# Two groups' gating moved out of PSUM and five pairs' exponentials written block by block: a new order for a chunked-attention and gated-convolution kernel

## The chip, the cores and the metric

The program runs on one core of one Trainium2 chip. The metric is device time in microseconds (us). The core has five instruction queues: TensorE (PE, matrix multiplies; its weight loads are shown as PEld), VectorE (DVE), ScalarE (ACT), GpSimd (POOL) and SyncE (SP), which issues the transfers. Each queue runs its instructions strictly in the order in which the program holds them; semaphores make one queue wait for another.

## The reference, cut to what matters

Attention inside chunks of 64 positions, then a gated causal convolution with two 512 x 512 matrices. Sizes: batch 8, 8 heads, 576 positions, head width 64; 8 x 576 = 4608 rows of width 512.

```python
scores = scale * (q_c @ k_c^T)                # per chunk of 64 and head
attn = exp(scores - max(scores))              # over the keys
attn = attn / (sum(attn) + 1e-09)
x = attn @ v_c                                # then heads side by side: rows x 512
gate_pre = sum over 5 taps of conv_w[k] * x shifted by 4-k rows (zeros before a batch)
gate = 1 / (1 + exp(-gate_pre))
out = (gate * (x @ w_val)) @ w_out
```

## The kernel before

The 4608 rows are cut into nine groups g of 512 rows. For each group the work is split into pieces with short names, and one long string, ORDER, lists all pieces of the whole program in one sequence. Every piece issues its instructions to fixed engines, in that sequence, so ORDER sets the queue of every engine. A letter D or G behind a name puts the piece on DVE or POOL instead of its usual engine. A second table, SLOTS, says for every tile of a ring (x, acc, ps, gate and so on) which of its buffers it takes; a buffer is taken again when the last reader of its former tile is done. All instructions are recorded by one helper, so in the profile all of them have its line, L160.

The pieces, with g the group, p the pair of head blocks (0 or 1), m and c blocks of 128 channels:

- Loads on SP: lq, lk, lv (q, k, v of a pair), lw (a quarter of a weight matrix), lc (convolution weights). st stores 128 rows of the result.
- Weights arrive as 64-bit numbers and are split into a high and a low part for the fp32r matmuls: w1 to w9, wa, wb, on DVE, ACT and POOL. v stands for w_val, o for w_out.
- S (PE): scores of a pair, tile s in PSUM, 128 x 1024, in two halves. mx (DVE): maximum of each of 16 blocks of 64 keys. sb (DVE): s minus the maximum, to the SBUF tile e_row. ex (ACT): one exp over all 1024 columns. sm (DVE): sum of each block, a 128 x 1040 reduction with the 1e-9 in its last column, and the reciprocal. nm (POOL): multiply by it, to en.
- T (PE): eight transposes to PSUM tile et. ec (ACT): copy to SBUF, eb. A (PE): times v, into two ps tiles u = 0, 1.
- xc, xr (ACT): copies of these to x (for the convolution) and, rounded, to xh. xd (DVE): the remainder, xl.
- k0 (ACT) and k .. 1 to k .. 4 (DVE): the five taps, in acc. sg (ACT): sigmoid, to gate.
- V (PE): x times w_val, four channel steps c of three matmuls each (xh with v_hi, xh with v_lo, xl with v_hi), in a ps tile. gm (DVE): gt = ps times gate.
- gr (ACT): gt rounded to gh. gd (POOL): the rest, gl. P (PE): times w_out, four steps c of three matmuls. oc (ACT): copy to o, which st stores.
- W: matmuls on a zero tile that nothing reads.

PSUM holds one s tile and one et tile (two banks each) and four ps tiles. V keeps its ps tile from its first matmul until gm has read it.

Of the kernel before, what the change touches and what calls it, by code (L numbers as in the profile page):

```python
# [514 lines left out]
```

## Time and profile before

| | |
|---|---|
| median of 3 runs | 305.24 us (304.71 to 305.42) |
| the profiled execution's own time | 305.96 us |
| span from its first to its last instruction | 304.2 us |
| mean granted TensorE clock | 0.988 of full speed |
| busy: PE, DVE, ACT, POOL | 274.9, 266.1, 185.2, 85.5 us |

How to read it. In the timeline a row begins with its start in us from the start of the span, then its length in us, then engine, line, operation, out<-in, and the count of equal instructions merged into it; in brackets stands the idle time of the engine before it and what ended it. A group of the list by shapes gives count, total busy us and mean ns of one, then the idle time before its instructions. A row's length counts from its own start to its own end; successive instructions of one engine overlap by some 0.07 to 0.1 us, and the matmuls by more, so what an instruction costs its queue is the distance to the next start. In a table of windows each engine has busy us and, in brackets, its number of instructions; PEclk is the granted TensorE clock.

### The profile page before, as it was taken

The numbers are of one execution on the slowest core, as the hardware profiler recorded it, in microseconds if no ns is written. First come the engines' busy times: TensorE is split into PE (matmuls) and PEld (weight loads), VectorE is DVE, ScalarE is ACT, GpSimd is POOL, SyncE is SP. The second block draws the span as 40 slices with busy tenths as digits, with TensorE's granted clock in tenths as the row PEclk, the third lists the DMA queues.
The fourth block names the chain that finished last, engine by engine and source line by source line (L and its number), as shares of the span: only waits on it lengthen the run. The fifth ranks groups of instructions, "written<-read, shape, count | busy, mean of one in ns | idle before, by whom it ended". The sixth has DMA issues, their size and how long they took to land.

```text
span 304.2 us, 7897 instructions
## 1 busy us (share of the span) xinstructions
PE 274.9 (90%) x3356; PEld 218.4 (72%) x3361; DVE 266.1 (87%) x374; ACT 185.2 (61%) x314; POOL 85.5 (28%) x77
## 2 busy tenths in 40 slices
...
DMA packets 14291, 42.47 MB, mean 140 GB/s; under 512 B 1712, under 2 KB 1712, under 8 KB 14256
## 3 DMA queue, kind: packets, MB, share of 16 engines
...
q14 instruction: 9, 0.07, 0.1%
...
## 4 chain that ended last, share of the span: by engine, by line
PE 57%; DVE 31%; DMA 5%; issue 4%; SPq 1%; ACT 1%; DVEq 0%; ACTq 0%
PE ps L160 50%; DVE acc L160 12%; PE s L160 4%; DVE gt L160 4%; DVE e_row L160 4%; DVE rs L160 3%; DVE mx L160 3%; DVE xl L160 2%; DMA kt<-in_k 2%; PE et L160 2%; DMA vt<-in_v 2%; DVE gate L160 1%; SPq L160 1%; DVE gl L160 0%; DVE v_lo L160 0%
## 5 line engine op out<-in xcount | busy, mean ns | idle before, releaser
L160 DVE SCALAR_TENSOR_TENSOR acc<-x,cw,acc 128x516 f32<-128x516 f32 (+1 forms) x144 | 113.1, 818 | 2.9 <-ACT acc L160 1.8
L160 POOL TENSOR_TENSOR gl<-gt,gh 128x512 fp32r<-128x512 f32 x24 | 32.7, 1365 | 149.5 <-ACT gh L160 149.5
L160 PE MATMUL ps<-xh,v_hi 128*128 128x512 f32 x144 | 59.5, 413 | 6.2 <-DVE xl L160 6.2
L160 PE MATMUL ps<-xl,v_hi 128*128 128x512 f32 x144 | 57.3, 398 | 3.1 <-DVE xl L160 3.1
L160 PE MATMUL ps<-o_hi,gh 128*128 128x512 f32 x144 | 58.4, 405 | 0.0
L160 PE MATMUL ps<-xh,v_lo 128*128 128x512 f32 x144 | 57.2, 397 | 0.0
L160 PE MATMUL ps<-o_lo,gh 128*128 128x512 f32 x144 | 56.9, 395 | 0.0
L160 PE MATMUL ps<-o_hi,gl 128*128 128x512 f32 x144 | 56.9, 395 | 0.0
L160 ACT ACTIVATE gate<-acc 128x512 f32<-128x512 uint32 (+8 forms) x72 | 30.3, 466 | 20.9 <-DVE acc L160 20.7
L160 POOL TENSOR_TENSOR en<-e_row,rs 128x1024 f32<-128x1024 f32 x16 | 32.4, 2022 | 23.0 <-DVE rs L160 22.5
L160 PEld LDWEIGHTS ps<-xh,v_hi 128*128 128x128 f32 x144 | 27.2, 189 | 13.1 <-DVE xl L160 6.6
L160 ACT COPY o<-ps 128x512 f32<-128x512 f32 x27 | 15.7, 584 | 32.1 <-PE ps L160 30.3
L160 PEld LDWEIGHTS ps<-xl,v_hi 128*128 128x128 f32 x144 | 27.2, 189 | 10.4 <-DVE xl L160 3.9
L160 PE MATMUL s<-kt,qt 64*64 64x64 f32 x1152 | 23.5, 231 | 12.3 <-DMA kt<-in_k 10.1
L160 PEld LDWEIGHTS s<-kt,qt 64*64 64x64 f32 x1152 | 20.8, 144 | 17.1 <-issue 15.5
L160 PEld LDWEIGHTS ps<-o_hi,gl 128*128 128x128 f32 x144 | 27.1, 188 | 6.5
L160 PEld LDWEIGHTS ps<-o_hi,gh 128*128 128x128 f32 x144 | 27.1, 188 | 6.5 <-issue 0.2
L160 PEld LDWEIGHTS ps<-xh,v_lo 128*128 128x128 f32 x144 | 27.4, 190 | 5.5
L160 PEld LDWEIGHTS ps<-o_lo,gh 128*128 128x128 f32 x144 | 27.1, 188 | 5.8
L160 ACT CAST gh<-gt 128x512 fp32r<-128x512 f32 x36 | 22.1, 618 | 13.7 <-DVE gt L160 13.5
L160 ACT ACTIVATE e_row<-e_row 128x1024 f32<-128x1024 f32 x18 | 19.1, 1061 | 17.8 <-DVE e_row L160 17.7
L160 ACT CAST xh<-ps 128x512 fp32r<-128x512 f32 x36 | 20.8, 592 | 14.8 <-PE ps L160 14.3
...
## 6 DMA issues: line engine op xcount, KB each, us to landing
...
```

The lines of the kernel that those rows point to most:

```text
L160: return tc.keep_in_program_order(fn(*args, **kwargs))
```

## The change

Only ORDER and SLOTS differ; the pieces' functions are the same in both files, and some of them were not used before. What the new order does:

- For pairs (0,1), (1,0), (1,1), (2,0) and (2,1) the pieces sb, ex and sm give way to ng, ea and rc. ng (DVE) multiplies the 128 x 16 maxima by -1/8. ea (ACT) is 16 ACTIVATE instructions of 128 x 64 that read s in PSUM, take a column of the maxima as bias, and write their row sums through the accumulator output. rc (DVE) adds 1e-9 to the 16 sums and takes the reciprocal.
- For groups 0 and 1 gm gives way to vc (ACT: copies the ps tile of V to SBUF) and gs (DVE; one of the eight on POOL): gt = that copy times gate.
- Other pieces change engine: ec of 0 0, 0 1 and 6 1, xc of the first group and other copies, some weight pieces, k0, nm and gd now stand on DVE where they stood on ACT or POOL, or the other way round. As a whole DVE has 15 gd (12 before), 4 nm (2), 7 oc (9), 6 xc (5); POOL has 14 nm (16) and 21 gd (24).
- Rings: gate has 8 buffers (6 before), o 3 (2), xh and xl 4 (3).
- All pieces are put in another sequence, the loads too.

```diff
...
-w2 v 2,sb 0 1,T 0 0,w4 v 2,ex 0 1,W 6,w4 v 3,w5 v 3,w7 v 2,sm 0 1,ec 0 0,w8 v 2,S 1 0 0,w6 v 3,A 0 0,w1 o 2,w1 o 0,
-gm 0 0,w8 o 1,mx 2 0,gr 0 0,V 0 2 0,k0 1 1,V 0 2 1,gdD 0 0,sg 0 3,V 0 2 2,xd 1 0 1,wa o 1,ec 1 1,V 0 2 3,gm 0 1,
...
+w7 v 1,S 0 1 1,w6 v 1,w3 v 2,W 15,ex 0 0,w8 v 1,mx 0 1,lq 1 1,w2 v 2,wa v 1,ng 0 1,sm 0 0,ea 0 1,nmD 0 0,w1 v 3,
+V 1 1 3,vc 0 1,gs 0 0,sg 0 1,S 3 1 0,k 1 2 1,S 3 1 1,sg 0 2,A 2 0,gs 0 1,gr 0 0,lq 4 1,vc 1 1,k 0 3 4,gr 0 1,
...
-    gate="0123450123450134343013250413250143201543021534201543",
+    gate="0123456701450623152473152064731526047315204673125046",
-    xh="012012012012021021",
+    xh="012301230123013201",
-    o="010110111110100110000110111001011010",
+    o="012020002212012021121021012012121201",
```

The functions that the new order calls:

```python
def ng(g, p):
    m = mxs[g, p]
    run(V.tensor_scalar, out=m, in0=m, scalar1=-SCALE, scalar2=None, op0=ALU.mult)

def ea(g, p):
    probs[g, p] = e_rows[next(e_slot)]
    rss[g, p] = r = tile_of("rs", [P, 16], F32)
    sb, m = flat(s_ps[g, p]), mxs[g, p]
    for j in range(16):
        run(S.activation, out=probs[g, p][:, j, 0:D], in_=sb[:, j], func=AF.Exp, bias=m[:, j:j + 1], scale=SCALE,
            accum_out=r[:, j:j + 1])

def rc(g, p):
    r = rss[g, p]
    run(V.tensor_scalar, out=r, in0=r, scalar1=1e-9, scalar2=None, op0=ALU.add)
    run(V.reciprocal, out=r, in_=r)

def vc(g, m, copy=S.copy):
    v_sb[g, m] = tile_of("gl", [P, T], F32R).bitcast(F32)
    run(copy, out=v_sb[g, m], in_=v_ps[g, m])

def gs(g, m, on=V):
    gt[g, m] = tile_of("gt", [P, T], F32)
    run(on.tensor_tensor, out=gt[g, m], in0=v_sb[g, m], in1=gate[g, m], op=ALU.mult)
```

DVE's queue at the softmax of pairs (0,1) and (1,0), before (the digit behind a tile's name is its buffer, the number behind the underscore its place in the program; rs is the row sums, xl the remainder of x):

```order
L160 TENSOR_REDUCE mx2_394<-s0_294 128x16
L160 TENSOR_TENSOR xl0_401<-ps0_312,xh0_371 128x2x256
L160 TENSOR_TENSOR e_row0_63<-s0_294,mx2_394 128x16x64
L160 TENSOR_SCALAR gt0_406<-acc1_130 128x512
L160 TENSOR_TENSOR v_lo_67<-gate5_201,gate4_199 128x512
L160 SCALAR_TENSOR_TENSOR gt0_406<-gate3_348,gt0_406 128x512
L160 TENSOR_REDUCE rs2_439<-e_row0_63 128x16
L160 RECIPROCAL rs2_439<-rs2_439 128x16
```

and now, at the same place:

```order
L161 COPY eb0_306<-et0_286 128x1024
L161 TENSOR_SCALAR rs0_265<-rs0_265 128x16
L161 RECIPROCAL rs0_265<-rs0_265 128x16
L161 TENSOR_REDUCE mx2_383<-s0_310 128x16
L161 TENSOR_SCALAR mx2_383<-mx2_383 128x16
L161 COPY x0_81<-ps1_350 128x2x256
L161 TENSOR_TENSOR gate5_212<-gt0_235,v_hi_65 128x512
L161 COPY x0_81<-ps0_349 128x2x256
L161 COPY eb1_435<-et0_418 128x1024
```

The 1024-column subtraction and reduction are gone from DVE; small operations on 16 columns and three kinds of copies stand there.

ACT's queue around the exps of pairs (1,0) and (1,1), before (eb is the copy of the transposes, xh the rounded x):

```order
L160 ACTIVATE e_row0_63<-e_row0_63 128x16x64
L160 ACTIVATE acc2_437<-x0_74,cw_69 128x512
L160 COPY eb1_459<-et0_427 128x1024
L160 ACTIVATE acc2_437<-x0_74,cw_69 128x512
L160 ACTIVATE gate4_504<-acc1_130 128x512
L160 COPY x0_74<-ps3_468 128x2x256
L160 COPY x0_74<-ps2_467 128x2x256
L160 CAST xh1_519<-ps2_467 128x2x256
```

and now:

```order
L161 ACTIVATE e_row0_63,rs2_398<-s0_310,mx2_383 128x64 x16
L161 CAST xh0_481<-ps0_349 128x2x256
L161 CAST v_hi_65<-gt0_437 128x512
L161 CAST xh0_481<-ps1_350 128x2x256
L161 ACTIVATE gate4_526<-acc1_187 128x512
L161 CAST xh1_533<-ps2_439 128x2x256
L161 COPY x0_81<-ps3_440 128x2x256
L161 ACTIVATE e_row1_64,rs1_539<-s0_483,mx0_528 128x64 x16
L161 CAST xh1_533<-ps3_440 128x2x256
```

The casts to xh, for which DVE's xl and then PE's V wait, stand directly behind 16 small ACTIVATEs in ACT's queue.

## Rows read from the trace of the kernel before

**Rows 1.** The page, busy time by engine.

```profile
PE 274.9 (90%) x3356; PEld 218.4 (72%) x3361; DVE 266.1 (87%) x374; ACT 185.2 (61%) x314; POOL 85.5 (28%) x77
```

**Rows 2.** Table of windows: window, length, busy us by engine, PEclk, DMA, GB/s.

```profile
40.00:50.00 10.00, 3.88 (x79) 2.65 (x78) 9.97 (x16) 4.00 (x8) 2.17 (x1) 0.87 0.01 2
50.00:60.00 10.00, 9.62 (x97) 7.77 (x98) 9.97 (x15) 7.58 (x12) 3.21 (x2) 0.79 0.72 245
...
170.00:180.00 10.00, 8.92 (x160) 7.25 (x159) 9.97 (x13) 8.20 (x17) 3.06 (x3) 1.00 0.68 230
...
220.00:230.00 10.00, 10.00 (x49) 8.21 (x48) 9.70 (x14) 6.31 (x13) 0.00 (x0) 1.00 0.49 182
```

**Rows 3.** Timeline of PE, 43 to 59 us, and the last matmul.

```profile
50.38 0.79 PE L160 MATMUL ps<-xh,v_hi 128*128 128x512 f32 x1 [6.20 <-DVE xl L160]
...
58.53 0.39 PE L160 MATMUL ps<-xh,v_hi 128*128 128x512 f32 x1
...
59.23 0.39 PE L160 MATMUL ps<-xh,v_hi 128*128 128x512 f32 x1
...
300.14 0.40 PE L160 MATMUL ps<-o_hi,gl 128*128 128x512 f32 x1
```

**Rows 4.** Timeline of DVE, 12 to 66 us.

```profile
11.99 1.23 DVE L160 TENSOR_REDUCE mx<-s 128x16 f32<-128x1024 f32 x1 [1.87 <-PE s L160]
...
48.38 0.68 DVE L160 TENSOR_TENSOR o_lo<-gate,gate 128x512 fp32r<-128x512 f32 x1
48.98 0.74 DVE L160 SCALAR_TENSOR_TENSOR acc<-x,cw,acc 128x512 f32<-128x512 f32 x1
49.64 0.68 DVE L160 TENSOR_TENSOR xl<-ps,xh 128x512 fp32r<-128x512 f32 x1
...
61.25 0.68 DVE L160 TENSOR_TENSOR gt<-ps,gate 128x512 f32<-128x512 f32 x1
61.84 1.41 DVE L160 TENSOR_SCALAR gt<-acc 128x512 uint32<-128x512 uint32 x1
...
65.52 0.69 DVE L160 TENSOR_TENSOR xl<-ps,xh 128x512 fp32r<-128x512 f32 x1 [0.29 <-ACT xh L160]
```

**Rows 5.** Groups by shape: count, busy us, mean ns, idle before.

```profile
L160 DVE TENSOR_TENSOR e_row<-s,mx 128x1024 f32<-128x1024 f32 x18 | 21.9, 1218 | 0.3
L160 DVE TENSOR_REDUCE rs<-e_row 128x16 f32<-128x1040 f32 x18 | 22.1, 1226 | 0.0
L160 DVE RECIPROCAL rs<-rs 128x16 f32<-128x16 f32 x18 | 4.6, 253 | 0.6
L160 DVE TENSOR_SCALAR gate<-gt 128x512 uint32<-128x512 uint32 x8 | 3.3, 410 | 0.0
L160 PE MATMUL s<-kt,qt 64*64 64x64 f32 x1152 | 23.5, 231 | 12.3 <-DMA kt<-in_k 10.1 <-DVE acc L160 1.1 <-PE ps L160 0.9
L160 PE MATMUL et<-ident,en 128*128 128x128 f32 x144 | 18.8, 273 | 0.9 <-POOL en L160 0.5 <-ACT eb L160 0.4
L160 ACT COPY o<-ps 128x512 f32<-128x512 f32 x27 | 15.7, 584 | 32.1 <-PE ps L160 30.3 <-issue 1.7
L160 ACT ACTIVATE e_row<-e_row 128x1024 f32<-128x1024 f32 x18 | 19.1, 1061 | 17.8 <-DVE e_row L160 17.7
L160 ACT ACTIVATE gate<-acc 128x64 f32<-128x64 f32 x8 | 2.0, 247 | 1.3 <-DVE acc L160 1.1
L160 ACT ACTIVATE gate<-acc 128x512 f32<-128x512 f32 x8 | 5.1, 637 | 4.9 <-DVE acc L160 4.9
L160 ACT ACTIVATE acc<-x,cw 128x512 f32<-128x512 f32 x7 | 4.8, 713 | 0.0
L160 ACT ACTIVATE cw_t<-cw_t 128x20 f32<-128x20 f32 x1 | 0.2, 220 | 0.7 <-DVE cw_t L160 0.7
```

**Rows 6.** Timeline of POOL, 60 to 63 us.

```profile
60.47 1.27 POOL L160 TENSOR_TENSOR gl<-gt,gh 128x512 fp32r<-128x512 f32 x1 [3.11 <-ACT gh L160]
61.70 1.27 POOL L160 TENSOR_TENSOR o_lo<-gate,gate 128x512 fp32r<-128x512 f32 x1
```

More of the change, by code (lines that the diff above doesn't have):

```diff
@@ new lines @@
+lk 4 1,w5 o 1,mx 1 1,lq 2 0,wa v 3,xr 0 1 0,xc 0 1 1,ng 1 1,xd 0 1 0,ea 1 1,nm 1 0,xd 0 0 1,xcD 0 1 0,w1 o 3,hl 1,
+T 1 0,wbD v 3,V 0 3 0,w4 o 1,W 2,wbD v 1,w7 o 1,V 0 3 1,w1 o 2,xr 0 1 1,w3 o 3,S 2 0 0,rc 1 1,w2 o 2,lw o 0,
+xd 0 1 1,S 2 0 1,nm 1 1,w6 o 1,w8D o 1,k0 0 2,V 0 3 2,lk 2 1,mx 2 0,lq 2 1,w2 o 3,V 0 3 3,lv 1 1,w5 o 2,W 4,lq 3 0,
+w4 o 3,ec 1 0,ng 2 0,k 0 2 1,k0 0 1,A 1 0,w7 o 3,ea 2 0,k 0 0 2,V 0 0 0,k 0 1 1,V 0 0 1,w8D o 3,V 0 0 2,waD o 1,
+k 0 1 2,k 0 2 2,w1 o 0,w3 o 2,xr 1 0 0,k 0 0 3,S 2 1 0,w6 o 3,S 2 1 1,rc 2 0,vc 0 3,xd 1 0 0,nm 2 0,V 0 0 3,lk 3 0,
@@ new lines @@
+xc 1 0 1,mx 2 1,lv 2 0,V 0 2 0,xr 1 0 1,lq 3 1,vc 0 0,T 1 1,xd 1 0 1,k0 0 3,waD o 3,ec 1 1,w4 o 2,wb o 3,w3 o 0,
+xc 1 0 0,A 1 1,k 0 0 4,w2 o 0,wb o 1,k 0 2 3,V 0 2 1,xr 1 1 0,lv 3 0,ng 2 1,w4 o 0,V 1 3 0,xr 1 1 1,k 0 3 1,ea 2 1,
+T 2 0,xd 1 1 0,V 0 2 2,k 0 3 2,V 1 3 1,xd 1 1 1,k 0 2 4,V 1 3 2,w7 o 2,V 1 3 3,k 0 3 3,V 0 2 3,w7 o 0,k 0 1 3,
+w5 o 0,S 3 0 0,w8D o 2,xc 1 1 0,S 3 0 1,rc 2 1,k0 1 0,w8D o 0,V 1 2 0,lk 3 1,xc 1 1 1,lq 4 0,mx 3 0,nm 2 1,V 1 2 1,
+w6 o 0,V 1 2 2,k0 1 1,sb 3 0,V 1 1 0,vc 0 2,k0 1 2,V 1 2 3,waD o 0,ec 2 0,V 0 1 0,k 1 0 1,V 1 1 1,vc 1 2,wbD o 0,
@@ new lines @@
+k0 2 2,k 1 3 1,P 0 3 0,k 1 0 4,oc 0 0,P 0 3 1,ec 3 0,k 1 3 2,st 0 0,P 0 3 2,lk 4 0,k 1 2 3,k0 2 1,P 0 3 3,k 2 0 1,
+sg 1 0,P 0 2 0,k 1 2 4,oc 0 3,P 0 1 3,k0 2 3,k 1 1 3,P 0 2 1,xr 2 1 1,k 1 3 3,oc 0 1,P 0 2 2,k 2 1 1,sg 1 2,st 0 1,
+P 0 2 3,gs 1 0,k 2 1 2,A 3 0,oc 0 2,k 1 1 4,gr 1 0,st 0 2,S 4 0 0,xr 3 0 0,lv 4 0,gs 1 2,S 4 0 1,sg 1 1,lv 3 1,
+k 1 3 4,V 2 1 0,lq 5 0,xd 2 1 1,V 2 1 1,hl 3,sg 1 3,k 2 1 3,V 2 1 2,gr 1 2,k 2 1 4,V 2 0 0,mx 4 0,gd 1 2,V 2 0 1,
+ex 3 1,V 2 0 2,xd 3 0 0,gsG 1 1,V 2 0 3,xc 3 0 1,sb 4 0,xr 3 0 1,V 2 1 3,gd 1 0,gr 1 1,xd 3 0 1,S 4 1 0,xc 3 0 0,
@@ new lines @@
+sm 3 1,S 4 1 1,ex 4 0,gd 1 1,P 1 3 0,P 1 2 0,gs 1 3,P 1 2 1,nmD 3 1,gr 1 3,P 1 3 1,P 1 3 2,sm 4 0,gd 1 3,T 3 1,
+sg 2 1,P 1 3 3,k 2 3 1,ec 3 1,gm 2 1,P 1 2 2,nm 4 0,oc 1 3,mx 4 1,P 1 2 3,A 3 1,oc 1 2,k 2 0 2,st 1 2,P 1 0 0,
+k 2 2 1,xc 3 1 0,lk 5 0,T 4 0,k 2 0 3,xr 3 1 0,gr 2 1,k 2 3 2,P 1 0 1,xc 3 1 1,xd 3 1 0,P 1 0 2,gd 2 1,k0 3 2,
+sb 4 1,P 1 0 3,V 2 3 0,k 2 3 3,oc 1 0,V 2 3 1,xr 3 1 1,k 2 2 2,st 1 0,V 2 3 2,k0 3 3,lv 5 0,k 2 3 4,lq 5 1,V 2 3 3,
+k 2 0 4,sg 2 3,V 2 2 0,k 2 2 3,sg 2 0,V 2 2 1,k 3 3 1,ec 4 0,V 2 2 2,gm 2 0,V 2 2 3,k0 3 0,k 3 2 1,gr 2 0,P 1 1 0,
@@ new lines @@
+k 2 2 4,P 1 1 1,k 3 3 2,sg 2 2,P 1 1 2,xd 3 1 1,hl 4,gd 2 0,gm 2 3,P 1 1 3,S 5 0 0,ex 4 1,gm 2 2,A 4 0,k 3 0 1,
+oc 1 1,S 5 0 1,gr 2 3,k 3 3 3,lv 4 1,V 3 3 0,k0 3 1,st 1 3,sm 4 1,gd 2 3,V 3 3 1,lq 6 0,xc 4 0 0,lk 5 1,xr 4 0 0,
+V 3 3 2,gr 2 2,k 3 3 4,V 3 3 3,xd 4 0 0,gd 2 2,P 2 3 0,mx 5 0,P 2 3 1,sg 3 3,nm 4 1,P 2 3 2,sb 5 0,xc 4 0 1,P 2 3 3,
+xr 4 0 1,V 3 0 0,xd 4 0 1,oc 2 3,k 3 1 1,T 4 1,st 2 3,k 3 0 2,V 3 0 1,ec 4 1,gm 3 3,V 3 0 2,k 3 0 3,A 4 1,k 3 2 2,
+S 5 1 0,k 3 1 2,xc 4 1 0,lv 5 1,S 5 1 1,k 3 0 4,xr 4 1 0,lk 7 1,V 3 0 3,xc 4 1 1,lk 6 0,xd 4 1 0,st 0 3,V 3 2 0,
@@ new lines @@
+xr 4 1 1,k 3 1 3,gr 3 3,V 3 1 0,mx 5 1,sg 3 0,gd 3 3,V 3 1 1,V 3 2 1,gm 3 0,k 3 1 4,V 3 1 2,gr 3 0,k0 4 2,sb 5 1,
+V 3 2 2,gd 3 0,P 2 1 0,xd 4 1 1,S 6 0 0,k 3 2 3,ex 5 1,S 6 0 1,k 3 2 4,V 3 1 3,lk 6 1,ex 5 0,sm 5 1,lq 6 1,V 4 3 0,
+V 4 3 1,sm 5 0,V 4 3 2,nm 5 1,sg 3 1,V 4 3 3,sg 3 2,V 3 2 3,mx 6 0,nm 5 0,k0 4 3,P 2 1 1,gm 3 1,P 2 1 2,gm 3 2,
+gr 3 1,P 2 1 3,sb 6 0,gr 3 2,hl 5,P 3 3 0,k0 4 0,T 5 1,gdD 3 2,k0 4 1,gdD 3 1,P 3 2 0,ec 5 1,k 4 3 1,P 3 3 1,oc 2 1,
+k 4 3 2,P 3 3 2,st 2 1,k 4 1 1,P 3 3 3,lq 7 0,k 4 2 1,T 5 0,oc 3 3,k 4 3 3,P 3 2 1,k 4 3 4,A 5 1,k 4 1 2,sg 4 3,
@@ new lines @@
+S 6 1 0,k 4 0 1,xc 5 1 1,S 6 1 1,xcD 5 1 0,P 3 2 2,lq 7 1,gm 4 3,xr 5 1 0,st 1 1,P 3 2 3,k0 5 2,lk 7 0,xd 5 1 0,
+P 3 1 0,lv 6 0,k 4 0 2,P 3 0 0,st 3 3,k0D 5 3,P 3 0 1,mx 6 1,ex 6 0,P 3 1 1,xr 5 1 1,k 4 0 3,P 3 1 2,ec 5 0,sm 6 0,
+P 3 1 3,oc 3 2,P 3 0 2,oc 3 1,st 3 2,xd 5 1 1,P 3 0 3,nm 6 0,sb 6 1,V 4 0 0,A 5 0,oc 3 0,k 4 0 4,ex 6 1,S 7 0 0,
+k 5 3 1,S 7 0 1,xc 5 0 0,k 5 2 1,xr 5 0 0,V 4 1 0,lk 8 1,k 4 2 2,xr 5 0 1,lv 6 1,V 4 1 1,k 4 1 3,xc 5 0 1,lq 8 0,
+T 6 0,xd 5 0 0,k0 5 0,V 4 1 2,k 4 2 3,gr 4 3,V 4 2 0,k 4 1 4,V 4 2 1,mx 7 0,gd 4 3,V 4 0 1,sg 4 1,V 4 0 2,xd 5 0 1,
@@ new lines @@
+ec 6 0,k 4 2 4,V 4 0 3,sg 4 0,k 5 3 2,V 4 2 2,sm 6 1,sg 4 2,P 2 2 0,V 4 1 3,gm 4 0,P 2 2 1,nm 6 1,sb 7 0,P 2 2 2,
+gr 4 0,k0 5 1,V 4 2 3,k 5 3 3,T 6 1,gdD 4 0,P 2 2 3,gm 4 2,S 7 1 0,k 5 1 1,gr 4 2,A 6 0,gm 4 1,gd 4 2,S 7 1 1,
+ecD 6 1,xr 6 0 0,V 5 3 0,lk 8 0,oc 2 2,hl 6,st 3 1,V 5 3 1,k 5 0 1,xc 6 0 1,st 2 2,V 5 3 2,k 5 3 4,lv 7 1,gr 4 1,
+xr 6 0 1,st 3 0,V 5 3 3,xcD 6 0 0,lq 8 1,sg 5 3,gdD 4 1,P 4 3 0,k0 6 0,gm 5 3,P 4 3 1,k 5 1 2,P 4 3 2,mx 7 1,
+P 4 3 3,P 4 0 0,xd 6 0 0,oc 4 3,P 4 0 1,sb 7 1,P 2 0 0,k 5 1 3,P 4 0 2,ex 7 0,k 5 2 2,P 2 0 1,gr 5 3,k 5 1 4,
@@ new lines @@
+P 2 0 2,ex 7 1,xd 6 0 1,P 2 0 3,k 5 0 2,V 5 1 0,oc 2 0,gdD 5 3,P 4 0 3,k0D 6 1,A 6 1,sm 7 0,sg 5 1,S 8 1 0,lv 7 0,
+S 8 1 1,xr 6 1 0,sm 7 1,nm 7 0,V 5 1 1,xr 6 1 1,xc 6 1 1,V 5 1 2,xd 6 1 0,oc 4 0,V 5 1 3,nm 7 1,xd 6 1 1,xc 6 1 0,
+st 4 0,V 5 0 0,mx 8 1,st 2 0,k0 6 2,P 4 1 0,gm 5 1,V 5 0 1,k 5 0 3,P 4 1 1,k 6 0 1,V 5 2 0,sb 8 1,T 7 0,V 5 0 2,
+k 5 0 4,V 5 0 3,k 5 2 3,sg 5 0,V 5 2 1,k0D 6 3,gr 5 1,k 6 3 1,V 5 2 2,ec 7 0,k 5 2 4,P 4 1 2,k 6 3 2,P 4 1 3,sg 5 2,
+gm 5 0,V 6 3 0,hl 7,gdD 5 1,gr 5 0,V 6 3 1,k 6 3 3,oc 4 1,V 6 3 2,st 4 1,k 6 3 4,V 6 3 3,st 4 3,gdD 5 0,sg 6 3,
@@ new lines @@
+A 7 0,k 6 0 2,S 8 0 0,gm 6 3,xr 7 0 0,V 5 2 3,k 6 0 3,xc 7 0 1,T 7 1,xd 7 0 0,xr 7 0 1,k 6 2 1,P 4 2 0,xc 7 0 0,
+ec 7 1,P 4 2 1,k0D 7 0,xd 7 0 1,P 4 2 2,k0 7 1,k 6 2 2,A 7 1,gm 5 2,k 6 1 1,S 8 0 1,gr 5 2,P 5 3 0,xr 7 1 0,gd 5 2,
+mx 8 0,xr 7 1 1,P 5 3 1,xc 7 1 1,xd 7 1 0,P 4 2 3,P 5 3 2,xd 7 1 1,xc 7 1 0,oc 4 2,k 6 2 3,P 5 3 3,k0 7 2,st 4 2,
+V 7 3 0,k 6 2 4,lv 8 1,k0 7 3,V 7 3 1,k 6 0 4,oc 5 3,V 7 3 2,k 7 3 1,gr 6 3,st 5 3,V 7 3 3,k 7 3 2,V 6 0 0,sb 8 0,
+gd 6 3,ex 8 1,V 6 0 1,V 6 0 2,sm 8 1,V 6 0 3,P 5 2 0,sg 6 0,k 7 3 3,V 6 2 0,gm 6 0,P 5 2 1,k 6 1 2,P 5 2 2,ex 8 0,
@@ new lines @@
+k 6 1 3,P 5 2 3,k 7 3 4,gr 6 0,V 6 2 1,oc 5 2,sm 8 0,V 6 2 2,st 5 2,V 6 1 0,lv 8 0,k 7 2 1,V 6 1 1,nmD 8 0,V 6 1 2,
+P 5 0 0,k 7 2 2,P 5 0 1,k 6 1 4,T 8 0,sg 6 1,hl 8,gd 6 0,V 6 1 3,ec 8 0,V 6 2 3,gm 6 1,sg 7 3,P 5 0 2,k 7 0 1,
+gr 6 1,P 5 1 0,nmD 8 1,sg 6 2,P 5 0 3,P 5 1 1,gm 7 3,gd 6 1,ocD 5 0,P 5 1 2,gm 6 2,A 8 0,gr 6 2,P 5 1 3,xcD 8 0 0,
+gr 7 3,gd 6 2,T 8 1,P 6 3 0,k 7 2 3,ec 8 1,P 6 3 1,k 7 0 2,oc 5 1,P 6 3 2,k 7 0 3,xc 8 0 1,st 5 1,P 6 3 3,st 5 0,
+k 7 0 4,k0 8 0,V 7 0 0,k 7 2 4,sg 7 0,V 7 0 1,k0D 8 1,xr 8 0 0,ocD 6 3,V 7 0 2,xr 8 0 1,xd 8 0 0,V 7 0 3,st 6 3,
```

122 lines of the change are left out of this document (34 added, 88 removed).

## The prediction, made before the changed kernel ran

> **What bounds the kernel now.** I read the busy sums first, then the table of windows and the timelines of the two engines that are full. PE is busy 274.9 of 304.2 us and DVE 266.1, ACT 185.2 [rows 1]. The windows show when: from 220 to 230 us PE is busy for all 10 us, while from 40 to 50 it is busy for 3.88, and DVE in that stretch for 9.97 [rows 2]. So the late part is set by PE, the early part by DVE: matmuls cannot start because the remainders xl that DVE makes come late. One such wait is 6.20 us, and the matmul behind it runs 0.79 us instead of 0.39, in a window with a granted clock of 0.79 [rows 2, 3]. From then on the program is a queue of PE work that has to be got through, up to 300.54 us [rows 3]. The time saved is therefore what the last late xl of the early part gains, less what PE then has more behind it.
>
> That point is the xl of group 1, second pair, second half (xd 1 1 1): DVE starts it at 65.52 us [rows 4]. Behind it, in both programs, stands one V step that needs it; all W matmuls stand ahead of it.
>
> **DVE ahead of that point.** The distance between starts is 0.60 us for a two-input operation of 512 columns (48.38 to 48.98) and 0.66 for a tap (48.98 to 49.64) [rows 4]. Operations of 1024 columns take 1.22 us [rows 5], less the same overlap of 0.08 us: 1.14. A sum with its reciprocal, 1226 and 253 ns [rows 5], comes to 1.43. Counted in both queues up to xd 1 1 1, the new one has less: 4 sb (4.6 us), 3 sm (4.3), 5 taps (3.3), 3 gm, one gd and one wb (5 x 0.60 = 3.0), together 15.2. It has more: one mx (1.1), two eb copies of 1024 columns from PSUM, priced like the subtraction that reads PSUM (2.3), three x copies and two w8 (3.0), one k0 (0.5), one weight step (0.3), and 13 operations on 16 columns, 5 in ng and 4 x 2 in rc. These have the reciprocal's row, 253 ns less overlap, 0.19 each: 2.5. Sum 9.7. Net 5.5 us less.
>
> By these prices DVE had 53.1 us of work ahead of that xl and began it at 65.52, so 12.4 us were lost: 6.0 before the first maximum at 11.99, whose wait for PE is in its row, and 6.4 in between. Part of the 6.4 is GpSimd: a TENSOR_SCALAR of 512 columns takes 1.41 us where its group has 0.41, beside a POOL operation from 61.70 to 62.97, while the PSUM reader in front of it, beside the POOL operation at 60.47, takes its usual 0.68 [rows 4 to 6]. In the new order the first maximum has 4.6 us of work before it and cannot come earlier than the same four 512 KB loads allow, so 7.4 are lost there. For the rest I followed the queue by hand.
>
> **The exps on ACT.** No row shows a 64-column ACTIVATE with bias column and accumulator. Nearest: 247 ns for 64 columns from SBUF; a column operand adds 713 - 637 = 76 ns at 512 columns; two neighbours overlap by 0.10 us; an accumulator output is at least free and at most a second instruction as long as a 20-column ACTIVATE, 220 ns [rows 5]. Bounds: 0.15 us (247 less overlap) and 0.47 (247 + 220). I take 0.30: 0.247 + 0.076 - 0.10 = 0.22 and 0.08 for the accumulator, nearer its cheap end because it writes one column. A pair then costs ACT 16 x 0.30 = 4.8 us instead of 1.06 [rows 5]. What hides it: ACT has idle time early, 6.0 of 10 us from 40 to 50 [rows 2]. What is queued behind it: the casts to xh, the copies to x and eb. DVE's xl waits for xh, PE's A for eb. Followed by hand at 0.30: ea 0 1 from 16.3 to 21.1, when DVE reaches rc 0 1 at 21.9; ea 1 0 from 23.9 to 28.7, xh at 29.2, when DVE is free at 29.0; ea 1 1 from 32.4 to 37.2, rc reached at 37.2; ea 2 0 from 42.1 to 46.9, rc reached at 47. The two engines meet within half a microsecond each time: the cover is just thick enough, and every 0.05 us more per instruction costs 3 pairs x 16 x 0.05 = 2.4 us before the point. On the walk DVE reaches xd 1 1 1 at 55.9; with 0.6 for the later start of the first maximum and 1.0 for collisions with POOL, 57.5. That is 8.0 earlier than 65.52: 5.5 of work and 2.5 of lost time.
>
> The Trainium skill, "ScalarE: Activation LUTs", What ACT_TABLE_LOAD costs, gives an ACTIVATE with a column bias about 280 ns + 0.833 ns per column, back-to-back ones overlapping by some 93. For 64 columns that is an estimate of 240 ns, without the accumulator; the 247 ns row agrees with the page's other form. By it a pair costs 3.8 us, ACT is never late, and only the 0.4 us by which it now holds DVE goes: 298.8.
>
> **PE behind that point.** Ahead of its V step the old queue had 18 V and 1 P steps, the new one 13 V: 6 more steps remain, each 0.70 us (58.53 to 59.23, three matmuls [rows 3]), 4.2 us. Half an S and one T fewer remain: 23.5 / 36 = 0.65 and 18.8 / 18 = 1.04 [rows 5]. Net 2.5 us more.
>
> **The rest.** vc adds 8 copies of 0.58 us [rows 5] to ACT and frees the ps tile without waiting for the sigmoid; off the path while ACT is not the bound. gs for gm: same 0.60 us if undisturbed; disturbed is a rival below. The longer rings only remove waits (bounds 0 and the half microsecond or so that a wait for a buffer would show). After the point I keep the losses of before, less 0.5 us: 46 long POOL operations instead of 53. The other engine moves there cancel: DVE's total by these prices falls by 1.6 us.
>
> **Sum.** -8.0 + 2.5 - 0.5 = -6.0 us. The profiled execution took 305.96 (span 304.2), 0.72 above the median 305.24. 305.24 - 6.0 = 299.2 us.
>
> **Rivals.**
> - ACT becomes the bound (slower). At 0.47 us an instruction a pair costs 7.5 us, 2.7 more; three pairs stand in series ahead of xd 1 1 1 (1 0, 1 1, 2 0): 8.2 us later, 307.4. It decides from 6.0 / 48 = 0.125 above 0.30, that is 0.425. For it: the cover is thin and a small instruction's time is nearly all fixed, 247 ns for 64 columns against 637 for 512 [rows 5]. Against: nothing in the rows makes a column's write cost as much as an instruction. 0.15.
> - GpSimd takes it back. The eight gs read two SBUF tiles where gm read PSUM. If the seven on DVE each meet a POOL operation, they stretch by about what was seen, up to 1.0 us each, 0.6 on average: 4.3 us, 303.5. For it: the 1.41 us row [rows 4, 6]. Against: gm's row beside POOL shows that POOL pieces can stand where DVE reads PSUM, and most of the early ones do in the new queue. The Trainium skill, "SBUF — State Buffer", Who interferes with whom, says that DVE operations with two SBUF inputs block against GpSimd operations that read SBUF, which speaks against gs; for one-input ones in a two-port mode it says the same, and the 1.41 us row agrees. 0.20.
> - All of it arrives. Exps at 0.25 or less and no collisions: DVE at 55.0 instead of 57.5, and 2.0 us of PE's idle time after 70 us go too (1.08 in the window of 170 to 180 alone [rows 2]): 294.7. 0.20.
> - It does nothing: the later groups, where DVE is as full as before, set the end whatever the start; 305. DVE still has all maxima, taps and remainders of groups 3 to 8. Against it: PE is busy for 10 us of 10 in the window of 220 to 230 [rows 2]. 0.05.
> - The forecast, 299.2, with its own range of 297 to 301.5: 0.40.
>
> **Chances and range.** No change means within 0.2%, 0.6 us, about what a measurement of this kernel can tell. Faster: 0.40 + 0.20 + 0.17 of the second rival = 0.77; same: 0.05; slower 0.18. The range of 8 in 10 leaves out most of the slower rival and the edge of the best: 293 to 305.
>
> **What would show it.** Right: the first long waits of PE for xl shrink; xd 1 1 1 starts at 56 to 59 us; 128x64 ACTIVATEs of e_row at about 0.3 us from start to start; PE without idle from 60 us on. Wrong: DVE or PE waiting for ACT's xh, eb or rs in the first 60 us with ACT full (first rival); gt<-gl rows far above 0.68 us beside POOL (second); PE idle after 70 us (fourth).

## The result and the profile after

The changed kernel takes 307.15 us (median of 12 runs, 305.48 to 308.74) where the kernel before takes 304.9 (12 runs). The ratio is 1.0068, 95% interval 1.0041 to 1.0095: slower by 0.7%. The forecast was 299.2. The profiled execution took 307.59 us with a span of 305.4.

The page, for [rows 1]: DVE has 9.3 us less, ACT 17.9 more, PE 6.3 more: 2.6 up to the end of xd 1 1 1, at a granted clock of 0.87 against 0.95 before, and 3.7 behind it.

```profile
PE 281.2 (92%) x3358; PEld 221.8 (73%) x3363; DVE 256.8 (84%) x380; ACT 203.1 (67%) x475; POOL 74.9 (25%) x71
```

The windows of [rows 2], and one more, 140 to 150 us.

```profile
40.00:50.00 10.00, 9.04 (x151) 6.16 (x152) 9.89 (x18) 9.68 (x43) 1.91 (x1) 0.89 0.63 207
50.00:60.00 10.00, 7.06 (x145) 5.97 (x146) 9.97 (x16) 8.17 (x26) 4.98 (x3) 0.83 0.58 217
140.00:150.00 10.00, 7.62 (x86) 6.13 (x85) 8.23 (x11) 8.18 (x12) 5.26 (x5) 0.83 0.53 195
170.00:180.00 10.00, 10.00 (x152) 8.46 (x145) 8.92 (x14) 8.93 (x17) 1.29 (x1) 1.00 0.47 162
```

ACT is now nearly full from 40 to 50, as its 16 small exps per pair make it. DVE is as full there as before. PE has no idle time from 170 to 180, where it had 1.08 us, but a hole from 140 to 150 that was not there.

DVE's timeline, for [rows 4]: the two operations of 16 columns that open rc, at 24 and 33 us; two places where a maximum is followed by ng; w8 at 43 us; an ng in its usual time; a weight step and two taps at 57 us; and the last late xl.

```profile
24.30 0.35 DVE L161 TENSOR_SCALAR rs<-rs 128x16 f32<-128x16 f32 x1
...
24.84 1.16 DVE L161 TENSOR_REDUCE mx<-s 128x16 f32<-128x1024 f32 x1
26.04 0.97 DVE L161 TENSOR_SCALAR mx<-mx 128x16 f32<-128x16 f32 x1
...
33.09 0.62 DVE L161 TENSOR_SCALAR rs<-rs 128x16 f32<-128x16 f32 x1
33.75 0.25 DVE L161 RECIPROCAL rs<-rs 128x16 f32<-128x16 f32 x1
33.92 1.16 DVE L161 TENSOR_REDUCE mx<-s 128x16 f32<-128x1024 f32 x1
35.11 1.80 DVE L161 TENSOR_SCALAR mx<-mx 128x16 f32<-128x16 f32 x1
...
43.00 2.00 DVE L161 TENSOR_TENSOR gate<-gate,gate 128x512 f32<-128x512 f32 x1
...
46.66 0.16 DVE L161 TENSOR_SCALAR mx<-mx 128x16 f32<-128x16 f32 x1
...
56.77 1.50 DVE L161 TENSOR_SCALAR gt<-acc 128x512 uint32<-128x512 uint32 x1
58.19 2.43 DVE L161 SCALAR_TENSOR_TENSOR acc<-x,cw,acc 128x512 f32<-128x512 f32 x2
...
63.14 0.68 DVE L161 TENSOR_TENSOR xl<-ps,xh 128x512 fp32r<-128x512 f32 x1
```

GpSimd's timeline beside them, for [rows 6].

```profile
25.07 1.90 POOL L161 TENSOR_TENSOR en<-e_row,rs 128x1024 f32<-128x1024 f32 x1 [0.46 <-DVE rs L161]
...
32.41 1.28 POOL L161 TENSOR_TENSOR gate<-gate,gate 128x512 f32<-128x512 f32 x1 [2.85 <-DVE gate L161]
...
34.98 1.90 POOL L161 TENSOR_TENSOR en<-e_row,rs 128x1024 f32<-128x1024 f32 x1
...
42.55 1.91 POOL L161 TENSOR_TENSOR en<-e_row,rs 128x1024 f32<-128x1024 f32 x1 [5.48 <-DVE rs L161]
...
56.33 3.08 POOL L161 TENSOR_TENSOR o_lo<-gate,gate 128x512 fp32r<-128x512 f32 x2 [0.87 <-DVE gate L161]
```

Read the two together. The ng of 16 columns that starts at 35.11 takes 1.80 us instead of 0.16; it ends at 36.91, GpSimd's product at 36.88. The ng at 26.04 ends at 27.01, the product at 26.97. The TENSOR_SCALAR of rc at 33.09 ends at 33.71, GpSimd's weight step at 33.69. The maxima at 24.84 and 33.92, which read PSUM, run beside the same GpSimd work in their usual time, and so does the reciprocal.

The point of the prediction, xd 1 1 1, is the last row: 63.14 us, against 65.52 before [rows 4] and 57.5 forecast. Up to it I sum two things: DVE's idle time (the window up to the start, less its busy time, 58.23 us before and 53.58 after), and, by rows, the length above an instruction's usual one where it is 0.15 us or more (forecast: 55.9 of the walk + 0.6 - 47.6 = 8.9 idle).

| up to xd 1 1 1, us | before | forecast | after |
|---|---|---|---|
| start | 65.52 | 57.5 | 63.14 |
| DVE idle | 7.3 | 8.9 | 9.6 |
| stretched beside GpSimd | 5.2 (5 operations) | 1.0 | 6.5 (7 operations) |
| the rest, its own work | 53.0 | 47.6 | 47.0 |

The seven are two ng (0.80 and 1.64), two rc (0.18 and 0.46), w8 at 43.00 (1.32), a weight step at 56.77 (1.08) and the taps at 58.19 (1.02). So 3.1 us fall on the operations of 16 columns and 3.4 on three of 512.

The exps on ACT, for the estimate of 0.30 us: timeline of ACT, then the groups by shape.

```profile
37.03 0.32 ACT L161 ACTIVATE e_row<-s,mx 128x64 f32<-128x64 f32 x1 [2.05 <-DVE mx L161]
37.24 0.19 ACT L161 ACTIVATION_READ_ACCUMULATOR e_row<-s,mx 128x1 f32 x1
37.34 0.31 ACT L161 ACTIVATE e_row<-s,mx 128x64 f32<-128x64 f32 x1
...
41.40 0.39 ACT L161 ACTIVATE e_row<-s,mx 128x64 f32<-128x64 f32 x1
41.59 0.29 ACT L161 ACTIVATION_READ_ACCUMULATOR e_row<-s,mx 128x1 f32 x1
41.69 0.67 ACT L161 CAST xh<-ps 128x512 fp32r<-128x512 f32 x1
```

```profile
L161 ACT ACTIVATE e_row<-s,mx 128x64 f32<-128x64 f32 x80 | 23.8, 351 | 6.6 <-DVE mx L161 6.6
...
L161 DVE TENSOR_TENSOR gt<-gl,gate 128x512 f32<-128x512 f32 x7 | 4.9, 694 | 0.0
```

From start to start an exp takes 0.29 us with its accumulator read, a pair 4.66 (37.03 to 41.69). The price held. ACT stood 2.05 us idle before this pair, behind the ng at 35.11. The gs, gt<-gl, have 694 ns: they were not hit.

PE's timeline at the hole, for [rows 3]. It is the one idle stretch after 66 us; before there were four there, 2.5 us together.

```profile
141.85 0.39 PE L161 MATMUL ps<-o_hi,gl 128*128 128x512 f32 x1
144.61 1.98 PE L161 MATMUL s<-kt,qt 64*64 64x64 f32 x64 [2.38 <-DMA kt<-in_k]
146.53 0.79 PE L161 MATMUL ps<-xh,v_hi 128*128 128x512 f32 x1
```

SP's queue ahead of it (the length of a merged row runs to the end of its last issue).

```profile
127.45 0.46 SPq L161 DMA_DIRECT2D kt<-in_k  x1
...
135.60 0.33 SPq L161 DMA_DIRECT2D vt<-in_v  x1
135.99 2.17 SPq L161 DMA_DIRECT2D kt<-in_k  x2
```

The waiting scores are S 6 0. Their load lk 6 0 is the second of the two at 135.99: the new order loads lk 7 1 first, into the buffer that S 5 0 had left, and lk 6 0 into the one that S 5 1 was still reading. It is issued at about 137.7 and lands 6.9 us later. The scores then take 1.98 us, where those at 135.33 us took 1.11: the granted clock, 0.83 over the window, was 0.50 from 144.61 to 146.59, its lower level, 1.2 of 2.4 GHz; PE had stood idle for 2.38 us before. From these scores to the fifth matmul behind them 3.61 us pass (144.61 to 148.22), for the same pieces at 135.33 it is 2.08: the lower clock cost 1.5.

### The profile page after: what moved, and what is told of

It is laid out like the page before. It is cut to its first block, busy times and chain, and to the rows that moved or that the text cites. A ratio compares the mean times of both kernels' runs of the same rounds, so it can differ in the third digit from the quotient of the medians.

```text
span 305.4 us, 8047 instructions
## 1 busy us (share of the span) xinstructions
PE 281.2 (92%) x3358; PEld 221.8 (73%) x3363; DVE 256.8 (84%) x380; ACT 203.1 (67%) x475; POOL 74.9 (25%) x71
## 4 chain that ended last, share of the span: by engine, by line
PE 76%; DVE 10%; DMA 7%; ACT 3%; SPq 2%; issue 1%; ACTq 0%
PE ps L161 67%; PE s L161 5%; PE et L161 4%; ACT e_row L161 3%; DMA acc<-in_moe_w_out 3%; DVE mx L161 2%; DMA qt<-in_q 2%; DMA kt<-in_k 2%; DVE acc L161 2%; DVE gate L161 2%; SPq L161 2%; DVE gt L161 1%; DVE xl L161 1%; DVE rs L161 1%; DVE eb L161 0%
## 5 line engine op out<-in xcount | busy, mean ns | idle before, releaser
L161 DVE SCALAR_TENSOR_TENSOR acc<-x,cw,acc 128x516 f32<-128x516 f32 (+1 forms) x144 | 105.7, 769 | 0.6
L161 PE MATMUL ps<-xh,v_hi 128*128 128x512 f32 x144 | 60.6, 421 | 0.0
L161 PE MATMUL ps<-xl,v_hi 128*128 128x512 f32 x144 | 58.0, 403 | 0.2 <-DVE xl L161 0.2
L161 PE MATMUL ps<-xh,v_lo 128*128 128x512 f32 x144 | 58.1, 403 | 0.0
L161 POOL TENSOR_TENSOR gl<-gt,gh 128x512 fp32r<-128x512 f32 x21 | 29.2, 1393 | 73.9 <-ACT gh L161 73.9
L161 POOL TENSOR_TENSOR en<-e_row,rs 128x1024 f32<-128x1024 f32 x14 | 27.2, 1948 | 61.8 <-DVE rs L161 48.5
L161 ACT COPY o<-ps 128x512 f32<-128x512 f32 x29 | 17.1, 590 | 31.0 <-PE ps L161 26.3
L161 ACT ACTIVATE e_row<-s,mx 128x64 f32<-128x64 f32 x80 | 23.8, 351 | 6.6 <-DVE mx L161 6.6
L161 DVE TENSOR_TENSOR xl<-ps,xh 128x512 fp32r<-128x512 f32 x36 | 24.0, 678 | 4.6 <-ACT xh L161 4.5
```

The costliest lines, as they stand in the source:

```text
L161: return tc.keep_in_program_order(fn(*args, **kwargs))
```

## The experiments

All were run against the kernel before on the same chip, in three groups: k_early, ng_act, whole_exp and before_block (its median there 305.12 us); both, both_wb, nm_dve and before_vc (305.33); nm_first and nm_dve_k (304.95). Beside the changed kernel it had 304.9, so a difference between kernels of two groups is known to some 0.4 us.

**k_early: the load moved (and lk 7 1 put behind it).**

```diff
-xc 4 0 0,lk 5 1,xr 4 0 0,
+xc 4 0 0,lk 5 1,lk 6 0,xr 4 0 0,
...
-xr 4 1 0,lk 7 1,V 3 0 3,xc 4 1 1,lk 6 0,xd 4 1 0,
+xr 4 1 0,V 3 0 3,xc 4 1 1,xd 4 1 0,
...
-k0 5 2,lk 7 0,xd 5 1 0,
+k0 5 2,lk 7 0,lk 7 1,xd 5 1 0,
...
-    kt="010101000001011110",
+    kt="010101000001010101",
```

> The changed kernel with one load moved: lk 6 0 stands right behind lk 5 1, in the other kt buffer, and lk 7 1 behind lk 7 0. Theory (late load): from 66 us on PE has one idle stretch, 2.38 us at 144.61, in which the scores of pair (6,0) wait for their k, and the matmuls behind it run at the lower clock; both go, -2.4 to -4.0 us, 303.2 to 304.8 us, PE busy 10.00 from 140 to 150 us. Rival (next in line): PE runs at once into the next late tap, remainder or load, and the gain is under 1 us, 306 to 307 us.

Measured: 304.83 us (304.09 to 305.85), 2.3 less than the changed kernel; against before 0.9995 (0.9979 to 1.0011). SP issues the load 10 us earlier, and the window has no hole:

```profile
127.70 0.91 SPq L159 DMA_DIRECT2D kt<-in_k  x2
```

```profile
140.00:150.00 10.00, 10.00 (x103) 7.97 (x102) 9.90 (x14) 9.44 (x14) 5.25 (x5) 1.00 0.27 95
```

The wait for k was a loss of its own: the theory, its gain just short of its range; 1.30 us of idle time came up at 169 us instead. Of the 2.3 us only 2.0 lie in the span (median 305.05 in the changed kernel, 303.05 here). The rest stands outside it: all runs of the changed kernel and of ng_act take 2.10 to 2.19 us longer than their span, those of k_early 1.74 to 1.84 and those of the kernel before 1.73 to 1.84. whole_exp, with the late load, has 1.74 to 1.86, so the load is not the reason; what is, stays open.

**ng_act: ng on ACT.**

```diff
-        run(V.tensor_scalar, out=m, in0=m, scalar1=-SCALE, scalar2=None, op0=ALU.mult)
+        run(S.mul, m, m, -SCALE)
```

> The changed kernel with ng (maxima times -1/8, 128 x 16) on ACT instead of DVE. Theory (GpSimd beside small DVE operations): DVE's ng stood 0.80 and 1.64 us behind a GpSimd en product, with ACT idle; both go, the exps of pair (1,0) start 0.7 us earlier, those of (1,1) some 2.3 us earlier, the remainder xd 1 1 1 at 60.5 to 61.5 us instead of 63.14, and the program is 1.5 to 2.5 us shorter, 304.6 to 305.6 us. Rival (the block goes to the next operation): the en products then hold the DVE operations behind, or PE is bound by its own earlier waits, and the time stays within 0.6 us of 307.15 us.

Measured: 304.30 us (301.83 to 307.48), 0.997 of before (0.9944 to 0.9996). xd 1 1 1 starts at 61.34, 1.8 us earlier. Behind the second maximum stands a PSUM reader now, and it runs beside the same GpSimd product, which starts at 34.71:

```profile
33.65 1.16 DVE L161 TENSOR_REDUCE mx<-s 128x16 f32<-128x1024 f32 x1
34.73 1.27 DVE L161 TENSOR_TENSOR xl<-ps,xh 128x512 fp32r<-128x512 f32 x2
```

The theory held. Not all of the 2.44 us by which the two ng had been stretched came back: an operation with two SBUF inputs behind the first maximum met GpSimd instead (0.68 us where it met nothing), and rc of pair (1,0) took 0.93 us instead of 0.62.

```profile
26.79 1.01 DVE L161 TENSOR_TENSOR gate<-gt,v_hi 128x512 f32<-128x512 f32 x1
```

The gain of the time, 2.85 us, is above its range, in runs that spread over 5.6 us. In the traced run the wait for k was 0.87 us instead of 2.38, so it is not all the collision's. With the early load the same edit brought 2.4 us (both against k_early).

**whole_exp: the block exps undone in the new order.** The diff shows pair (0,1); (1,0), (1,1), (2,0) and (2,1) likewise.

```diff
-wa v 1,ng 0 1,sm 0 0,ea 0 1,nmD 0 0,
+wa v 1,sb 0 1,sm 0 0,ex 0 1,nmD 0 0,
...
-S 1 0 1,rc 0 1,w5 o 3,
+S 1 0 1,sm 0 1,w5 o 3,
...
```

> The changed kernel with the block exps undone: sb, ex, sm in the places of ng, ea, rc for the five pairs. Theory (DVE's work counts): DVE has some 6.4 us more up to xd 1 1 1, less up to 3.1 us of stretched ng and rc, so xd 1 1 1 at 66 to 69 us and the time 309 to 312 us. Rival (ACT's hold of s is the loss): the scores of the next pair no longer wait 4.65 us for ACT, PE's waits of 0.83, 3.75 and 2.33 us at 32, 37 and 52 us shrink, and the time is 303 to 306 us.

Measured: 311.97 us, 1.0232 of before (1.0188 to 1.0275). xd 1 1 1 starts at 67.98, 4.8 us later than in the changed kernel, and the time is 4.8 us longer. In the new order the block exps are worth 4.8 us; ACT's hold of the s tile was not the loss. GpSimd stretched three operations of DVE up to there, 3.6 us, instead of seven: the w8, the weight step and the taps again, while the places of ng and rc are undisturbed. This subtraction ran beside the product that GpSimd began at 25.79, this sum beside the weight step from 33.38 to 34.65, both in their usual time:

```profile
26.75 1.23 DVE L159 TENSOR_TENSOR e_row<-s,mx 128x1024 f32<-128x1024 f32 x1
...
33.76 1.23 DVE L159 TENSOR_REDUCE rs<-e_row 128x16 f32<-128x1040 f32 x1
```

**before_block: the block exps alone, in the old order.** Again pair (0,1) of five.

```diff
-w2 v 2,sb 0 1,T 0 0,w4 v 2,ex 0 1,W 6,w4 v 3,w5 v 3,w7 v 2,sm 0 1,ec 0 0,
+w2 v 2,ng 0 1,T 0 0,w4 v 2,ea 0 1,W 6,w4 v 3,w5 v 3,w7 v 2,rc 0 1,ec 0 0,
...
```

> The kernel before with ng, ea, rc in the places of sb, ex, sm for the same five pairs, nothing else changed. Theory (DVE's work counts): DVE has 6.4 us less up to xd 1 1 1, less some 2 us of small operations stretched beside GpSimd; xd 1 1 1 at 60 to 62 us instead of 65.52, the time 301 to 303 us against 304.9 before. Rival (ACT's hold of s and of its queue is the loss): the next scores wait for the 16 exps, ACT's xh and eb come late, and the time is 305 to 309 us.

Measured: 328.48 us, 1.0763 of before (1.0733 to 1.0792). The theory failed, and the rival had the mechanism but less than a fifth of its size. The old order has little between exp and sum, and between one pair's exp and the next pair's scores. DVE waits for the sums and then for the scores, and PE for the s tile:

```profile
23.69 0.17 DVE L159 TENSOR_SCALAR rs<-rs 128x16 f32<-128x16 f32 x1 [3.45 <-ACT e_row L159]
...
28.08 1.23 DVE L159 TENSOR_REDUCE mx<-s 128x16 f32<-128x1024 f32 x1 [1.85 <-PE s L159]
...
35.77 0.17 DVE L159 TENSOR_SCALAR rs<-rs 128x16 f32<-128x16 f32 x1 [2.33 <-ACT e_row L159]
```

```profile
35.79 1.13 PE L159 MATMUL s<-kt,qt 64*64 64x64 f32 x32 [4.57 <-ACT e_row L159]
...
83.44 1.14 PE L159 MATMUL s<-kt,qt 64*64 64x64 f32 x32 [9.58 <-ACT e_row L159]
```

xd 1 1 1 comes at 75.15, 9.6 us late, and the 9.58 us at 83.44 come on top; the other 4 of the 23 us were not traced. So the same edit is worth -4.8 us in one order and +23 in the other.

**before_vc: vc and gs alone, in the old order.** The first of the eight blocks of groups 0 and 1:

```diff
-V 0 0 3,lq 3 0,
+V 0 0 3,vc 0 0,lq 3 0,
...
-gm 0 0,w8 o 1,
+gs 0 0,w8 o 1,
...
```

> The kernel before with vc (copy of V's result to SBUF on ACT, right behind V) and gs in the places of gm for the eight blocks of groups 0 and 1, the gl buffers numbered anew for it. Theory (off the path): ACT has idle time there and DVE's gs lasts as long as gm; within 0.6 us of the kernel before, 304.3 to 305.5 us. Rival (ps tiles come free earlier and PE runs ahead): 302 to 304 us. Second rival (gs reads two SBUF tiles and stands behind GpSimd): 305.6 to 308 us.

Measured: 309.81 us, 1.0151 of before (1.0132 to 1.017). Not off the path: in this order a vc stands at the head of ACT's queue until V is done (five of the eight wait, 7.9 us together), here 3.46 us, and holds the table load and the sigmoid behind it, for which DVE then waits 1.61 us. Of the eight gs, 956 ns in the mean, three stood behind GpSimd, by 0.86, 0.99 and 0.35 us: the second rival's mechanism, and the time is above its range.

```profile
54.56 0.59 ACT L159 COPY gl<-ps 128x512 f32<-128x512 f32 x1 [3.46 <-PE ps L159]
55.17 1.28 ACT L159 ACT_TABLE_LOAD   x1
```

```profile
57.12 0.69 DVE L159 TENSOR_TENSOR gt<-gl,gate 128x512 f32<-128x512 f32 x1 [1.61 <-ACT gate L159]
...
62.56 1.54 DVE L159 TENSOR_TENSOR gt<-gl,gate 128x512 f32<-128x512 f32 x1
```

How much of the 4.5 us is each isn't settled. The part undone in the new order was not tried: there PE's queue needs the ps tiles that vc frees.

**nm_dve and nm_dve_k: no GpSimd beside ng, but ng on DVE.**

```diff
-mx 1 0,nm 0 1,w2 o 1,W 4,w6 v 2,lv 1 0,ng 1 0,xcD 0 0 1,
+mx 1 0,w2 o 1,W 4,w6 v 2,lv 1 0,ng 1 0,nmD 0 1,xcD 0 0 1,
...
-ng 1 1,xd 0 1 0,ea 1 1,nm 1 0,xd 0 0 1,
+ng 1 1,nmD 1 0,xd 0 1 0,ea 1 1,xd 0 0 1,
```

> The changed kernel with nm of pairs (0,1) and (1,0) on DVE, each directly behind the next pair's ng, which stays on DVE. No GpSimd operation then stands beside ng; DVE has 2 x 1.14 us of work more and 2.44 us of stretching less. Theory (DVE's total up to xd 1 1 1 decides): the two cancel, xd 1 1 1 near 63 us, the time within 0.7 us of 307.15 us. Rival (the start of ACT's exps decides): they start 0.8 and 1.5 us earlier as with ng on ACT, and the time is 304 to 305.5 us.

> The kernel with nm of pairs (0,1) and (1,0) on DVE behind the next ng, and with the earlier k load, so that the wide spread of the former (302.89 to 309.55 us) is out of the comparison. Theory (DVE's total up to xd 1 1 1 decides, 2.28 us of work for 2.44 us of stretching): within 0.7 us of the changed kernel with the earlier k load, 304.83 us. Rival (the start of ACT's exps decides): 302 to 303.3 us.

Measured: nm_dve 1.0002 of before (0.9973 to 1.0031), in runs from 302.89 to 309.55 us, too wide to tell the two theories apart; so the second run, with the early load: 304.22 us (303.54 to 305.14), 0.6 less than k_early: within the theory's range and outside the rival's. The ng take 0.17 us, the exps of pairs (1,0) and (1,1) start at 26.34 and 35.75 instead of 27.34 and 37.24 in k_early, and xd 1 1 1 at 62.82 instead of 63.35. ACT's start gains 1.0 and 1.5 us, xd 1 1 1 0.5 and the time 0.6: it goes with DVE's total, not with ACT's start.

```profile
34.26 1.16 DVE L159 TENSOR_REDUCE mx<-s 128x16 f32<-128x1024 f32 x1
35.46 0.17 DVE L159 TENSOR_SCALAR mx<-mx 128x16 f32<-128x16 f32 x1
35.54 1.22 DVE L159 TENSOR_TENSOR en<-e_row,rs 128x1024 f32<-128x1024 f32 x1
```

**both and both_wb: the edits together, then two weight steps moved from GpSimd.** both is k_early with ng_act; both_wb in addition:

```diff
-wb o 3,w3 o 0,xc 1 0 0,A 1 1,k 0 0 4,w2 o 0,wb o 1,
+wbD o 3,w3 o 0,xc 1 0 0,A 1 1,k 0 0 4,w2 o 0,wbD o 1,
```

> The changed kernel with both edits, the earlier k load and ng on ACT. Theory (two separate losses, one before 66 us, one at 144 us): the gains add, 2.3 + 2.85 us, 302.0 us (301.5 to 302.6). Rival (they share: with ng on ACT the wait for k in the traced run was 0.87 us instead of 2.38 us): the earlier load brings at most 1 us more, 303.3 to 304.3 us.

> The kernel with both edits, and in addition the two additions wb of w_out's quarters 1 and 3 on DVE instead of GpSimd. Theory (GpSimd beside DVE costs DVE more than the work is worth): two operations of DVE stood 1.1 and 1.0 us behind these two; they go, for 2 x 0.60 us of new work, and the remainder xd 1 1 1 comes 0.9 us earlier; the time is 0.5 to 1 us below that of both edits. Rival (DVE's queue is not what PE waits for there): within 0.4 us of both edits.

Measured: both 302.46 us, 0.9922 (0.9895 to 0.9948); both_wb 301.63 us, 0.9886 (0.987 to 0.9901). The gains add to 4.7 of the 5.15 us, and the two weight steps bring another 0.8, as expected, though the two intervals overlap. xd 1 1 1 is at 60.23 and 59.46 us.

**nm_first: one more GpSimd collision removed.**

```diff
-xd 0 0 0,w8 v 3,xr 0 0 1,rc 1 0,
+xd 0 0 0,xr 0 0 1,rc 1 0,
...
-lq 2 0,wa v 3,xr 0 1 0,
+lq 2 0,xr 0 1 0,
...
-nm 1 0,xd 0 0 1,
+nm 1 0,w8 v 3,wa v 3,xd 0 0 1,
```

> The kernel with both edits and the two wb on DVE, and in addition w8 v 3 and wa v 3 behind nm 1 0 in GpSimd's queue. Theory (what is left of the loss before 66 us is GpSimd too): rc 1 0 no longer stands 0.73 us behind w8 v 3, the en product starts at 32 us instead of 33.78, PE's idle time of 4.04 us before the transposes of pair (1,0) shrinks by 1.7 us, xd 1 1 1 comes 0.5 to 1 us earlier than 59.46; the time is 0.5 to 1.5 us below that kernel's 301.63 us. Rival (DVE's own work and the scores' round trip through ACT bound it now, or the late v_lo takes the place): within 0.4 us of 301.63 us.

Measured: 301.51 us, 0.9885 (0.9859 to 0.9911), the same as both_wb: the rival. The rc is no longer stretched and PE's wait before the transposes falls from 4.04 to 2.48 us, but DVE then waits for the weight step that was moved back, and xd 1 1 1 stays at 59.91:

```profile
36.94 0.69 DVE L159 TENSOR_TENSOR v_lo<-gate,gate 128x512 fp32r<-128x512 f32 x1 [1.17 <-POOL gate L159]
```

## Why the prediction was wrong

**What held.** DVE's own work up to xd 1 1 1, 47.6 forecast, 47.0 measured. The exp, 0.30 us forecast, 0.29 measured; so the first rival (ACT the bound) fell with its price. Taking xd 1 1 1 as the point held too: whole_exp moved it by +4.8 us and the time by +4.8; among the kernels with the early load it went from 63.35 to 59.46 and the time from 304.83 to 301.63, 3.2 us for 3.9. That xd 1 1 1 came earlier at all is right, 2.4 us instead of 8.0. PE's long wait for an xl, 6.20 us [rows 3], is gone; its longest between 20 us and the point is now 3.75 us, for en of pair (1,0), which GpSimd makes.

**What failed first: the term "1.0 for collisions with POOL", 6.5 us measured.** It carries 5.5 of the 5.6 us by which xd 1 1 1 was later than forecast. Counted by the same rows, the old order had 5.2 us of it, nearly all of the 6.4 that the prediction found lost in between and put down to GpSimd only in part; the 1.0 rested on the view that GpSimd's early pieces mostly stand where DVE reads PSUM. Of the 6.5 us, 3.4 fall on w8, a weight step and taps, and whole_exp has them as well. The other 3.1 are new. Under them lies the price of the 13 small operations, 0.19 us each after the row of the reciprocal [rows 5]. The reciprocals kept their 253 ns. But ng and the first half of rc are TENSOR_SCALARs from SBUF to SBUF, the kind of the row of 1.41 us [rows 4], which I had read and applied to weight steps and to gs alone. What they replaced, the subtraction from PSUM and the 1040-column sum, ran beside GpSimd at full speed (whole_exp). So the change took cover away from DVE at the two places where GpSimd begins nm beside a maximum. The operation behind the maximum was the wrong one: nm lasts 1.9 us, the maximum that reads PSUM covers 1.2 of it, and ng meets the rest. The second rival (GpSimd takes it back) had the mechanism and about the size, but on gs; in the new order those were not hit.

That stretching delays xd 1 1 1 is shown for ng (ng_act, 1.8 us) and for the weight step and the taps (both_wb, 0.8). It is not shown for all of it: nm_first took 0.73 us more off rc and gained nothing.

The Trainium skill, "SBUF — State Buffer", Who interferes with whom, says that on this chip a tensor_reduce never contends with GpSimd, a tensor_scalar in a two-port mode does, and a tensor_tensor with both inputs in SBUF does. The traces agree in these rows: ng 1.80 us and w8 2.00, and in whole_exp the sum 1.23 beside GpSimd. Put to ng, its rule would have said so ahead of the run.

**What failed second: "after the point I keep the losses of before, less 0.5 us".** These are PE's windows from the end of xd 1 1 1 to the end of the last matmul, for before, the changed kernel and k_early.

```profile
66.21:300.54 234.33, 231.79 (x2616) 188.03 (x2615) 207.15 (x284) 145.50 (x249) 58.86 (x49) 1.00 0.35 121
63.82:301.69 237.87, 235.44 (x2591) 191.07 (x2591) 202.52 (x289) 155.73 (x283) 52.50 (x45) 0.99 0.31 110
64.03:299.34 235.31, 233.96 (x2591) 189.79 (x2591) 202.20 (x288) 155.64 (x283) 52.49 (x45) 1.00 0.31 111
```

The four idle stretches of before did go, but one wait of 2.38 us came from the order of loads: PE is idle for 2.4 us in place of 2.5. With it came the lower clock, which the sum had at nothing: 1.5 us, the busy time above k_early's. I had counted what DVE, ACT and PE have queued, and of SP's queue only the four loads ahead of the first maximum; in the new order S 6 0's load stands behind a load for S 7 1, which is needed later. The term "2.5 us more" of PE work held: k_early has 2.2 more than before, both at the full clock.

The sum with the measured sizes, for the profiled executions: -2.4 (the point) + 2.2 (PE work behind it) - 0.1 (idle behind it) + 1.5 (lower clock) + 0.4 (outside the span, see k_early) = +1.6 us, and they took 307.59 and 305.96. The medians differ by 2.25; the rest is the spread of single runs.

**What was not seen at all.** That the parts of the change lean on the order: alone in the old order the block exps cost 23 us and vc with gs 4.5. "Off the path while ACT is not the bound" was wrong as a reason: in before_vc an instruction that waits at the head of ACT's queue holds what stands behind it. What vc costs in the new order was not measured by itself.
